# Two layernormed tiles transposed by DMA instead of TensorE, with a reordered start of the loads

## Chip, cores, metric

The kernel runs on one core of one Trainium2 chip. The time is device microseconds of one execution; several executions are taken of each kernel and the median is quoted. Before the change it was 1510.9 us (three runs, 1510.87 to 1511.14). A profile adds a trace of one execution. Its span is about 2 us shorter than the time of the same execution, so spans are compared with spans and times with times.

## The reference

The program adds three things: the input, a recurrent attention over segments, and an MLP block. The change touches only the beginning of the MLP block.

```python
x = A_x                                   # (1, 2048, 1024) bf16
xn = _layernorm(x)
out = x + _A_ref(xn, ...) + _B_ref(xn, B_w1, B_w2, B_w3, B_w4)

def _B_ref(x, w1, w2, w3, w4):            # receives xn
    h = _gelu(_layernorm(x) @ w1)         # phase one of the kernel: h
    ...                                   # shifts of h along the sequence, @ w2, phase two
    x1 = x + hs
    return x1 + _gelu(_layernorm(x1) @ w3) @ w4
```

## The kernel before

Phase one handles 16 tiles of 128 rows (0 to 15). For each tile VectorE makes the statistics, then somebody writes the twice normalized tile `xn2`. TensorE needs it transposed, as the moving operand of the product with w1. Tiles 0 to 7 are normalized by VectorE and transposed by TensorE (eight 128-column matmuls with the identity, copied by ScalarE out of PSUM, the memory that the matmuls write to). Tiles 8 to 15 are normalized by ScalarE and transposed by a DMA.

```python
ring = p0.enter_context(tc.tile_pool(name="p0ring", bufs=3))
NPE = 8
load_x(0)
for c in range(4):                                     # w1 in four quarters, 524 KB each
    nc.sync.dma_start(w1_sb[:, 2 * c:2 * c + 2, :], w1_v[:, 2 * c:2 * c + 2, :])
    if c < 2:
        load_x(1 + c)
# ... x tiles 3 to 6, w2, x tiles 7 to 9 ...

def norm_stats(n, part=None):
    # ... bn_stats, bn_aggr and ab on VectorE, rr on GpSimd ...
    if n >= NPE:
        nc.gpsimd.tensor_scalar(nm2[:], mv[:, 0:1], rr[:, 1:2], -1.0, ...)

def norm2(n, xn2T, jj):
    xn2 = ring.tile([P, D], BF16, tag="xn2")           # three slots
    if n < NPE:
        nc.vector.tensor_scalar(xn2[:, c], xts[n][:, c], ...)           # L274
    else:
        nc.scalar.activation(xn2[:], xts[n][:], ACTF.Identity, ...)     # L276
        nc.sync.dma_start_transpose(xn2T[:, jj], xn2[:])
    return xn2

def norm1(n):                                          # the once normalized tile, kept
    nc.vector.tensor_scalar(xn_keep[n // 4][:, n % 4], xts[n][:], ...)
    # ... stored to memory by GpSimd's queue ...
    load_x(n + 10)

def stage1(n0, nt, xn2T, between, j0=0):
    for co in range(KT):                               # 8 column blocks
        ps = psum.tile([P, 512], F32, tag="mm", bufs=4)
        for k in range(KT):
            nc.tensor.matmul(ps[...], w1_sb[:, k, co * P:(co + 1) * P], xn2T[...], ...)
        nc.scalar.activation(hTB[...], ps[:, :w], ACTF.Gelu_apprx_tanh)  # frees the PSUM slot
        for f in between.get(co, ()):                  # transposes, normalizations of later tiles
            f()

def prep(n):
    norm2_of(n); norm_stats(n + 1); norm1(n - 2)
```

## Time and profile before

| what | before |
|---|---|
| median time | 1510.9 us (in the later comparison of six executions 1511.02) |
| span of the profile | 1508.97 us (rounded to 1509.0 on the page) |
| TensorE at work | 99% of the span |
| first product with w1 ends | 11.98 us |
| phase two (product with w2) begins | 67.47 us |
| last matmul ends | 1505.08 us |
| from there to the end of the span | 3.89 us |

The last rows come from the trace's records of TensorE. The stretch from the end of the first product to the beginning of phase two, 55.49 us, holds everything that the change touches except the load order. It is called *the stretch* below.

One view of the kernel before that the prediction does not show is needed later: ScalarE's instructions in order of time (start, length, engine, line, what, and in brackets an idle time and its releaser).

```profile
28.80 0.38 ACT L318 ACTIVATE hTB<-ps 128x256 bf16<-128x256 f32 x1 [0.23 <-PE ps L316]
29.07 1.23 ACT L276 ACTIVATE xn<-xt,nm,rr 128x1024 bf16<-128x1024 bf16 x1
30.21 0.37 ACT L318 ACTIVATE hTB<-ps 128x256 bf16<-128x256 f32 x1
```

L318 is the copy with GELU that frees a PSUM slot. L276 is the normalization of tile 8. It begins at 29.07 in between two such copies and delays the next by 1.2 us, which four PSUM slots absorb: TensorE shows no wait there.

### The profile page before, as it was taken

Reading aid. Unit: us, or ns where it says so; the run is one execution under the profiler, and the core shown is the slowest. Engines: PE = TensorE matmul, PEld = TensorE weight load, DVE = VectorE, ACT = ScalarE, POOL = GpSimd, SP = SyncE. Lnnn points to the kernel's source line nnn. Section 1 sums busy time; section 2 is a strip of 40 time slices with the busy share of each in tenths; the row PEclk is TensorE's granted clock in tenths of the full one; section 3 lists DMA queues with packets and bytes.
Section 4 is the critical chain, followed back from the end, with each engine's and each line's share of the span. In section 5 each row is a group of like instructions: output and inputs, shape, how many; then the busy total and the mean of one; then the engine's idle time right before and its main releaser. Section 6 shows DMA issues by size and latency. Waiting matters only on the chain.

```text
span 1509.0 us, 24273 instructions
## 1 busy us (share of the span) xinstructions
PE 1499.1 (99%) x9778; PEld 804.6 (53%) x9850; DVE 544.6 (36%) x1136; ACT 504.0 (33%) x1144; POOL 175.0 (12%) x245
## 2 busy tenths in 40 slices
PE   9999999999999999999999999999999999999998
PEld 8844444445444444444466645664665455545555
DVE  8382230100020212211246624651564166516641
ACT  6533103013012011111156614650663266416630
POOL 5241020211111221100000000001000100010001
PEclk9999999999999999999999999999999999999999
DMA  8699752363345877622389957992998299918921
GB/s 303 143 273 320 216 177 90 136 203 112 126 159 149 196 247 253 217 98 84 126 224 253 243 125 178 252 241 67 240 252 203 74 227 227 214 60 199 217 48 51
DMA packets 303251, 272.41 MB, mean 181 GB/s; under 512 B 153894, under 2 KB 270152, under 8 KB 303136
## 3 DMA queue, kind: packets, MB, share of 16 engines
q1 hardware_dynamic: 281248, 189.92, 51.1%
q0 software_dynamic: 21744, 80.83, 15.7%
q8 instruction: 79, 1.29, 0.4%
q14 instruction: 36, 0.29, 0.1%
q10 hardware_dynamic: 144, 0.07, 0.0%
HBM read 190.08 MB, written 45.29 MB: 156 GB/s over the span
## 4 chain that ended last, share of the span: by engine, by line
PE 98%; DMA 1%; issue 0%; SPq 0%; DVE 0%
PE ps L654 30%; PE pso L712 15%; PE ps L593 15%; PE ps L534 13%; PE ps L560 13%; PE ps L392 4%; PE ps L316 3%; PE psO L693 2%; PE psS L669 2%; PE ps L852 1%; PE ps L484 1%; DMA PT<-Pn 1%; PE gps L463 0%; PE ps L449 0%; DMA w_sb<-in_B_w_dram 0%
## 5 line engine op out<-in xcount | busy, mean ns | idle before, releaser
L654 PE MATMUL ps<-hTb,wt 128*128 128x396 bf16 (+2 forms) x2528 | 484.8, 342 | 0.0
L654 PEld LDWEIGHTS <-wt 128*128 128x128 bf16 x2528 | 236.8, 98 | 175.4
L593 PE MATMUL ps<-wt,xT 128*128 128x512 bf16 x1003 | 220.1, 379 | 1.1
L712 PE MATMUL pso<-wo_sb,oX 128*128 128x512 bf16 (+1 forms) x972 | 208.5, 372 | 1.1
L534 PE MATMUL ps<-xn3T,w_sb 128*128 128x512 bf16 x896 | 196.2, 379 | 0.0
L560 PE MATMUL ps<-w_sb,h3T 128*128 128x512 bf16 x873 | 194.3, 379 | 1.2
L593 PEld LDWEIGHTS <-xT 128*128 128x128 bf16 x1024 | 100.2, 98 | 120.8
L535 ACT ACTIVATE h3T<-ps 128x512 bf16<-128x512 f32 x112 | 66.8, 597 | 290.4 <-PE ps L534 289.5
L712 PEld LDWEIGHTS <-oX 128*128 128x128 bf16 x992 | 96.3, 98 | 107.4
L656 ACT CAST KT<-ps 128x462 bf16<-128x462 f32 (+2 forms) x160 | 81.7, 510 | 203.1 <-PE ps L654 199.0
L560 PEld LDWEIGHTS <-h3T 128*128 128x128 bf16 x896 | 87.0, 98 | 103.4
L534 PEld LDWEIGHTS <-w_sb 128*128 128x128 bf16 x896 | 86.6, 98 | 102.1
L675 DVE TENSOR_REDUCE sums<-sm 99x4 f32<-99x396 f32 (+2 forms) x176 | 97.6, 555 | 114.3 <-ACT sm L673 114.3
L658 ACT ACTIVATE QT<-ps 128x462 bf16<-128x462 f32 (+2 forms) x160 | 83.8, 524 | 120.4 <-PE ps L654 106.1
L595 ACT CAST Vs<-ps 128x512 bf16<-128x512 f32 x64 | 37.4, 585 | 233.2 <-PE ps L593 175.0
L671 DVE TENSOR_TENSOR sm<-psS,c_mask_reg_sb 99x396 f32<-99x396 f32 x152 | 86.7, 570 | 72.6 <-PE psS L669 72.4
L599 DVE CAST Vs<-ps 128x512 bf16<-128x512 f32 x64 | 44.3, 692 | 171.6 <-PE ps L593 163.2
L673 ACT ACTIVATE sm<-sm 99x396 f32<-99x396 f32 (+2 forms) x176 | 92.8, 527 | 34.7 <-DVE sm L671 27.9
L681 DVE TENSOR_TENSOR Pn<-sm,rs 99x396 bf16<-99x396 f32 (+2 forms) x176 | 98.9, 562 | 6.8 <-DMA PT<-Pn 0.9
L719 POOL DMA_DIRECT2D out_dram<-ot x30 | 16.4, 545 | 698.9 <-DVE ot L718 693.0
L561 DVE TENSOR_TENSOR R<-ps,R 128x512 f32<-128x512 f32 x32 | 21.9, 689 | 173.5 <-PE ps L560 156.8
L718 DVE TENSOR_TENSOR ot<-pso,Rt 128x512 bf16<-128x512 f32 (+1 forms) x33 | 22.2, 675 | 170.6 <-PE pso L712 166.5
(122 smaller groups left out, 1054.1 us busy)
## 6 DMA issues: line engine op xcount, KB each, us to landing
wt<-in_A_Wq_dram SPq DMA_DIRECT2D x76, 512.0 KB
wt<-in_A_Wk_dram SPq DMA_DIRECT2D x76, 512.0 KB
wt<-in_A_Wv_dram POOLq DMA_DIRECT2D x24, 1024.0 KB, 6.5
V_scratch<-Vs SPq DMA_DIRECT2D x32, 512.0 KB
V<-V_scratch SPq DMA_DIRECT2D x40, 384.0 KB
R_scratch<-x POOLq DMA_DIRECT2D x16, 512.0 KB, 3.5
R<-R_scratch SPq DMA_DIRECT2D x16, 512.0 KB
R_scratch<-R POOLq DMA_DIRECT2D x16, 512.0 KB, 3.1
```

The costliest lines, as they stand in the source:

```text
L534: nc.tensor.matmul(ps[:].rearrange("p (n t) -> p n t", t=P), w3_sb[:, k, f * P:(f + 1) * P], xn3T[tb][:, :, k, :], start=(k == 0), stop=(k ...
L535: nc.scalar.activation(h3T[:, f, :], ps[:], ACTF.Gelu_apprx_tanh)
L560: nc.tensor.matmul(ps[:], h3T[:, f, j * P:(j + 1) * P], w4_sb[:, f, ch * 512:(ch + 1) * 512], start=(f == 0), stop=(f == FT - 1))
L593: nc.tensor.matmul(ps[:], xT[:, m4 * 4 + j, k, :], wv[:, k, :], start=(k == 0), stop=(k == KT - 1))
L654: nc.tensor.matmul(ps[:, :nb], w[:, k, hh * P:(hh + 1) * P], B["hT"][:, k, :nb], start=(k == 0), stop=(k == KT - 1))
L656: nc.scalar.copy(dst[:, hh, :], ps[:, :nb])
L658: nc.scalar.mul(dst[:, hh, :], ps[:, :nb], scale)
L671: nc.vector.tensor_tensor(sm[:T, :, :T], S3, t["mask"][:].unsqueeze(1).to_broadcast((T, 4, T)), op=ALU.add)
L673: nc.scalar.activation(e[:T, :, :T], sm[:T, :, :T], ACTF.Exp, scale=LN2)
L675: nc.vector.tensor_reduce(ss, e[:T, :, :T], axis=AX.X, op=ALU.add)
L681: nc.vector.tensor_tensor(Pn[:T, :, :T], e[:T, :, :T], rs[:T, :].unsqueeze(2).to_broadcast((T, 4, T)), op=ALU.mult)
L712: nc.tensor.matmul(self.ps[:, :self.w], self.oX[0][:, h, self.oX[1] + self.gl * P:self.oX[1] + (self.gl + 1) * P], wo_sb[:, h, self.cc], s ...
```

## The change

The intent: take 16 transposing matmuls off TensorE, which is the bound (tiles 6 and 7 by DMA, still normalized on VectorE); load x tile 2 behind w1's third quarter so that TensorE gets that quarter sooner; and record the transposes of tiles 2 and 3 one column block earlier.

```diff
-                    NPE = 8
+                    NPE = 6
...
-                        if c < 2:
-                            load_x(1 + c)
+                        if c in (0, 2):
+                            load_x(1 + c // 2)
...
-                        if n >= NPE:
+                        if n >= 8:
                             nc.gpsimd.tensor_scalar(nm2[:], ...)
...
-                        if n < NPE:
+                        if n < 8:
                             ... nc.vector.tensor_scalar(xn2[:, c], ...)
                         else:
                             nc.scalar.activation(xn2[:], ...)
+                        if n >= NPE:
                             nc.sync.dma_start_transpose(xn2T[:, jj], xn2[:])
...
-                            stage1(n - 1, 1, ..., {7 - n: [lambda n=n: tr(n, 0)], 8 - n: [lambda n=n: tr(n, 1)]}, (n - 1) % 2)
+                            stage1(n - 1, 1, ..., {6 - n: [lambda n=n: tr(n, 0)], 7 - n: [lambda n=n: tr(n, 1)]}, (n - 1) % 2)
...
-                        if n0 == 4:
-                            for c in range(4):
-                                between[1 + 2 * c // 2 + (c > 1)] += [lambda c=c: tr(6 + c // 2, c % 2)]
```

More of the change, by code (lines that the diff above doesn't have):

```diff
@@ L351 @@
                     load_consts(4)
-                    for n in range(1, NPE):
+                    for n in range(1, 8):
                         if n > 1:
@@ L361 @@
                         elif n < 4:
-                            stage1(n - 1, 1, tiles2[(n - 1) // 2 * 2], {7 - n: [lambda n=n: tr(n, 0)], 8 - n: [lambda n=n: tr(n, 1)]}, (n - 1) % 2)
+                            stage1(n - 1, 1, tiles2[(n - 1) // 2 * 2], {6 - n: [lambda n=n: tr(n, 0)], 7 - n: [lambda n=n: tr(n, 1)]}, (n - 1) % 2)
                     stage1(3, 1, tiles2[2], {0: [lambda: tr(4, 0)], 2: [lambda: tr(4, 1)], 4: [lambda: tr(5, 0)], 5: [lambda: tr(5, 1)]}, 1)
```

## The prediction

Its sum: 1510.9 - 0.89 - 0.01 = 1510.0 us. The 0.89 rests on 55.8 ns per 128-column matmul, as in the trace before (starts 55 or 56 ns apart, 48 in 2.68 us). The 0.01 assumes that swapping two loads leaves the landing of w1's fourth quarter where it was, which was my estimate from the even landings of the quarters (9.67 and 11.03 us). This quarter landed 3.34 us after the second one before the change (7.69 to 11.03).

> **What bounds the kernel now.** I read the page's engine table and its chain first, then TensorE's waits, then the chain in order of time for the first 70 us, where the whole change lies.
>
> ```profile
> PE 1499.1 (99%) x9778; PEld 804.6 (53%) x9850; DVE 544.6 (36%) x1136; ACT 504.0 (33%) x1144; POOL 175.0 (12%) x245
> ...
> PE 98%; DMA 1%; issue 0%; SPq 0%; DVE 0%
> ```
>
> TensorE is on the chain for 98% of the span. The list of its waits is nearly empty in the first 130 us:
>
> ```profile
> PE warm L333 <- DVE wz L327: 1.4, 1, 1.4
> PE ps L306 <- DMA w_sb<-in_B_w_dram: 0.3, 1, 0.3
> PE ps L306 <- ACT xn2T L296: 0.2, 1, 0.2
> ```
>
> In the whole span there is only one more, of 0.2 us. So TensorE's own work sets the end: an instruction taken off TensorE takes its own length off the time, if no wait fills the hole. What TensorE does in phase one, with the length of each piece as second number (a chain of start, length, what):
>
> ```profile
> 3.17 6.50 DMA w_sb<-in_B_w_dram
> 9.67 0.05 issue
> 9.71 1.07 PE ps L306 x16
> 10.78 0.45 PE ps L293 x8
> 11.23 0.92 PE ps L306 x16
> ...
> 26.57 0.22 PE ps L293 x4
> 26.79 0.87 PE ps L316 x8
> 27.66 0.22 PE ps L293 x4
> 27.88 1.75 PE ps L316 x16
> 29.63 0.22 PE ps L293 x4
> 29.85 0.87 PE ps L316 x8
> 30.73 0.22 PE ps L293 x4
> 30.95 36.68 PE ps L316 x336
> ```
>
> L306 is the first product with w1, row block by row block, L293 the transposes, L316 the later products. The reader is to see two things. The four L293 pieces from 26.57 on are the transposes of tiles 6 and 7, each a hole of 0.22 us in a stream that otherwise never stops. And before 9.71 the chain runs back into a load: TensorE had been waiting for the third quarter of w1 for 0.3 us.
>
> When do the quarters land? The load queue (SP) tells it, since in the built kernel every issue waits for the landing of the eighth issue before it. Counting from x tile 0, the w2 loads wait for w1's second quarter, x tile 2, w1's third quarter and w1's fourth. The last three of them:
>
> ```profile
> 8.34 0.38 SPq L244 DMA_DIRECT2D w_sb<-in_B_w_dram  x1
> 9.69 0.37 SPq L244 DMA_DIRECT2D w_sb<-in_B_w_dram  x1
> 11.05 0.37 SPq L244 DMA_DIRECT2D w_sb<-in_B_w_dram  x1
> ```
>
> So x tile 2 landed just before 8.34, the third quarter at about 9.67 and the fourth at about 11.03. A quarter (524 KB) takes 1.36 us, some 386 GB/s, and the view of stretches shows the transfers saturated (shares of about 1.0) from 3.5 to 25.5 us.
>
> [...] The trace has 0.22 us for four, or 0.45 for eight: 55.8 ns[...]. [...] In the trace the transpose issued alone at 49.99 has its traffic from 51.0 to 52.5, with a peak of 291 GB/s in a half-microsecond slice[...].
>
> **The change part by part.**
>
> *Transposes of tiles 6 and 7 off TensorE.* The built kernel has 16 matmuls and 16 weight loads fewer. On the chain they are 4 pieces of 0.2232 us (4 x 55.8 ns), together 0.89 us. The pieces after them run on at the pace of 0.109 us per 256-column matmul on either side, so nothing hides the holes: minus 0.89 us. Four copies from PSUM on ACT (0.58 us each) go too; ACT is not on the chain, so 0.
>
> *Their two DMA transposes.* The inputs are still made on VectorE:
>
> ```profile
> 23.16 0.55 DVE L274 TENSOR_SCALAR xn<-xt,mv,rr 128x1024 bf16<-128x1024 bf16 x1
> ...
> 25.88 0.55 DVE L274 TENSOR_SCALAR xn<-xt,mv,rr 128x1024 bf16<-128x1024 bf16 x1
> ```
>
> These are tiles 6 and 7, ready at 23.7 and 26.4. The transpose issued alone later in this phase shows what comes then:
>
> ```profile
> 49.99 1.23 SPq L277 DMA_TRANSPOSE xn2T<-xn  x1
> ```
>
> 1.23 us to issue, and its bytes have moved by about 52.4: 2.4 us in all. Tile 6 meets the end of the saturated stretch, so I allow it until 27.5. Tile 7 has lighter traffic (half of the engines' time from 25.5, 0.9 from 26.5) and should land at 29.0 to 29.5. TensorE needs both when it begins the product of tiles 6 and 7. That product begins after the 64 matmuls of tiles 4 and 5: it begins at 24.81 (the chain has 32 matmuls from 23.92, the first 16 of them tile 3's at 55.8 ns), and 64 x 0.109 us and the four holes end at 32.7 now, hence at about 31.8 after the change. About 2.5 us to spare: 0. The queue stays in order, but the loads of x tiles 14 and 15 were issued at 25.3 and 28.0, just after the two issues end, and tile 15 is first read at 40.8.
>
> *Third x tile behind the third quarter.* The third quarter lands where x tile 2 used to leave off plus what the swap saves, at 9.67 minus 0.68 (262 KB at 386 GB/s), so at 9.0. The wait of 0.3 us ahead of it vanishes, the 16 matmuls begin at about 9.40, and with the 8 transposes of tile 1 TensorE is done at 10.75. There it wants the fourth quarter, and the same bytes stand before that one as before the change: 11.03. Before the change TensorE came to it at 11.05, just as it landed, so no wait shows. Now a wait of 0.3 us shows. The wait moves by one quarter, gain 0.0 to 0.03 us. X tile 2 lands at about 9.70 in place of 8.3; VectorE first turns to it at 9.67, and it waits 0.28 us for x tile 3 two microseconds later anyway, so the delay of some 0.05 us is swallowed.
>
> *Transposes of tiles 2 and 3 sooner.* They move ahead by one group of 8 matmuls (0.45 us). The same instructions run, and the inputs are long there: tile 2's is ready at 12.9 and is wanted at 14.4 (14.83 less 0.45). What it buys is room for the copy of tile 2's second half, which ends at 16.34 where TensorE reads it at 16.39. No wait is shown there now: gain 0.
>
> Sum: 1510.9 - 0.89 - 0.01 = 1510.0 us, a gain of 0.06%. Behind phase one everything is released by the progress of TensorE and shifts with it.
>
> **The rivals.** *The load wait really goes.* If the fourth quarter had landed well before 11.05, the swap would save 0.3 us more: 1509.7. For it: the profile shows no wait for that quarter. Against it: the issue at 11.05 that waits for its landing. *A DMA transpose takes the place.* If tile 7 landed after 31.8, TensorE would wait for it; at 32.7 the gain is gone (1510.9), and at 34 the kernel is 1.3 us slower (1512.2). For it: tile 6 is issued into saturated traffic, and tile 7's issue stands behind it and a load in one queue. Against it: more than 2 us to spare. *A later engine or transfer swallows the shift.* TensorE shows no wait after 12 us but one of 0.2 us, so a transfer that runs on its own clock would have to be nearly late now; then anything down to no gain (1510.9). *VectorE becomes the bound early.* It is busy for 9.4 to 9.7 of 10 us up to 40 us, and a late x tile 2 could push all normalizations back; tile 2's margin of 1.5 us would have to be used up first, and the time would then be about 1510.5.
>
> **Range and chances.** The three runs of before spread over 0.27 us. The first rival makes 1509.7 and partial losses 1510.5, so 1509.6 to 1510.5 should hold 8 in 10. Two per cent are 30 us. The change touches 1 us of TensorE's work, and no rival comes near 30 us: within 2% at 0.994, 0.003 for either side.
>
> **What would show the steps right or wrong.** Right: 48 in place of 64 transposes; TensorE's load wait of about 0.3 us still there, now ahead of the last 16 matmuls of L306; no wait ahead of the product of tiles 6 and 7; the next phase beginning about 0.9 us before its present 67.6. Wrong: a wait of TensorE for a DMA transpose near 32 us; the last 16 L306 matmuls beginning clearly before 11.0; VectorE's second tile statistics starting late by more than 0.3 us and TensorE waiting at a transpose; or a start of the next phase shifted by other than 0.8 to 1.0 us with the end shifted by another amount.

## More of the kernel before

Note the pools: `xn2` lives in a ring of three slots (buffers that are used again and again; a new tile must wait until the last reader of its slot is done), and the product's PSUM ring ("mm") has four.

## The result, and the profile after

The changed kernel took 1512.51 us in the median. Its six executions fall in two groups: 1511.77, 1511.99, 1512.40 and 1512.61, then 1514.79 (the profiled one) and 1514.82. The kernel before, measured on the same chip in the same rounds, had a median of 1511.02 (1510.82 to 1512.17). A ratio is the mean time of one kernel's runs over that of the other's of the same rounds, so it is not quite the ratio of the medians. Here it is 1.0011, with a 95% interval of 0.9998 to 1.0024: within 2%, as predicted, but 2.5 us above the predicted time, and even the fastest execution lies above the predicted range. The interval touches 1, so the times alone hardly show the loss. The profile shows it piece by piece.

The engine table of the page after, and the shares of the chain that ended last:

```profile
PE 1503.9 (99%) x9834; PEld 804.6 (53%) x9834; DVE 544.3 (36%) x1136; ACT 502.3 (33%) x1140; POOL 174.9 (12%) x245
...
PE 98%; DMA 1%; DVE 0%; issue 0%; POOL 0%; ACT 0%; POOLq 0%; DVEq 0%
```

Weight loads went from 9850 to 9834, as counted: 16 fewer, and ScalarE's instructions from 1144 to 1140. (The matmul counts, 9778 and 9834, can't be compared: the trace before lacks some records.) TensorE is still the bound, but GpSimd and ScalarE now stand in the list of the chain, which was not so before. TensorE's waits after (line waited in, releaser, total us, times, longest):

```profile
PE ps L317 <- ACT hTB L319: 2.0, 1, 2.0
PE warm L334 <- DVE wz L328: 1.4, 1, 1.4
PE psO L691 <- DMA PT<-Pn: 0.8, 1, 0.8
```

The first line is new. It is a wait of 2.0 us in the product with w1 (L317), and the releaser is a ScalarE copy, not a DMA. The load wait of before is gone from the list in this profile: TensorE started that product later, at 7.76 instead of 7.45, and the fourth quarter came earlier, at 10.75 instead of 11.03. The chain in order of time tells the story of the 2.0 us:

```profile
23.42 0.55 DVE xn L274
...
23.99 4.68 DMA xn2T<-xn
...
28.77 0.55 DVE xn L274
29.32 0.61 DVE st L262
...
29.96 0.22 DVE mv L263
...
30.20 0.23 DVE ab L264
...
30.58 0.88 POOL rr L265
...
31.55 0.28 POOL nm L267
...
31.85 0.05 ACT xn L276
...
33.00 0.37 ACT hTB L319
...
33.41 11.65 PE ps L317 x90
```

Read from the top: VectorE normalizes tile 6 (23.42). Its DMA transpose takes 4.68 us. Only when that has landed does VectorE normalize tile 7 (28.77). Then come the statistics of tile 8 on VectorE and GpSimd, ScalarE's normalization of tile 8, a ScalarE copy, and only then TensorE. VectorE's own view of the same time:

```profile
25.44 0.69 DVE L259 BATCH_NORM_STATS2 st<-xt 128x6 f32<-128x512 bf16 x1
28.77 0.55 DVE L274 TENSOR_SCALAR xn<-xt,mv,rr 128x1024 bf16<-128x1024 bf16 x1 [2.65 <-DMA xn2T<-xn]
```

VectorE stood still for 2.65 us, waiting for tile 6's DMA transpose before it wrote tile 7. The load queue's view after:

```profile
23.99 1.43 SPq L278 DMA_TRANSPOSE xn2T<-xn  x1
25.55 0.54 SPq L234 DMA_DIRECT2D xt<-in_A_x_dram  x1
29.35 1.40 SPq L278 DMA_TRANSPOSE xn2T<-xn  x1
```

The queue issued in the recorded order (23.99, 25.55, 29.35). Tile 7's transpose was issued at 29.35, where the prediction had its input ready at 26.4. Pairing issues with their completions in the trace, tile 6 landed at 28.68 and tile 7 at 32.23. ScalarE's view, against the one of before:

```profile
27.98 0.38 ACT L319 ACTIVATE hTB<-ps 128x256 bf16<-128x256 f32 x1 [0.49 <-PE ps L317]
31.85 1.24 ACT L276 ACTIVATE xn<-xt,nm,rr 128x1024 bf16<-128x1024 bf16 x1 [3.49 <-POOL nm L267]
33.00 0.91 ACT L319 ACTIVATE hTB<-ps 128x256 bf16<-128x256 f32 x3
```

ScalarE has tile 8's normalization next in its order, waits 3.49 us for it, and only at 33.00 makes three copies in a row. Until then the four PSUM slots are full and TensorE can't write.

TensorE stood from 31.44 to 33.41, and that had a sequel. Stretches of half a microsecond with TensorE's busy time, granted clock, DMA share and GB/s:

```profile
34.00:34.50 0.50, 0.50 (x7) 1.00 0.29 67
34.50:35.00 0.50, 0.50 (x6) 0.68 1.27 289
35.00:35.50 0.50, 0.50 (x4) 0.50 1.18 291
37.50:38.00 0.50, 0.50 (x5) 0.50 1.04 341
38.00:38.50 0.50, 0.50 (x6) 0.91 0.56 189
```

The third number from the right is the granted clock that the trace records, as a share of TensorE's full speed. From 34.67 to 38.09, for 3.413 us, it is at half: 256-column matmuls start 0.213 us apart there, and 0.109 us apart before and after. About half of 3.413 us, 1.7 us, is lost by my estimate. What decides whether a stop is followed by half clock is not shown here. In the changed kernel half clock follows a stop of 1.98 us; after stops of 1.89 us (e2_filled), 0.96 us (e6_tile8_later) and 0.75 us (e1b_both_own_place) in the experiments below none follows.

Where the 3.65 us between the two profiled executions are:

| piece | before | after | difference |
|---|---|---|---|
| start to end of first product | 11.98 | 11.78 | -0.20 |
| the stretch, to phase two | 55.49 | 58.23 | +2.74 |
| phase two to last matmul | 1437.61 | 1438.27 | +0.66 |
| last matmul to end of span | 3.89 | 4.35 | +0.46 |
| span | 1508.97 | 1512.63 | +3.65 |

(The differences are rounded one by one.)

The stretch splits into -0.89 (16 transposes), -0.17 (a gain at tile 2 that was predicted as 0, below), +1.98 (the wait), +0.17 (what a stop costs TensorE beyond the idle time, taken from the experiments below), and +1.65 left over, which matches the 1.7 of the half clock. Without the half clock it would be +1.09.

Where does the stop of VectorE come from? The list of the built program's instructions names what tile 7's normalization waits for. First the kernel before, then after:

```
54 L274 TensorScalarPtr xn_577<-xt_145,mv_555,rr_557 128x1024 [waits PE_49,Pool_49]
54 L274 TensorScalarPtr xn_578<-xt_145,mv_555,rr_557 128x1024 [waits DMAHW6_49,Pool_49]
```

Before, tile 7 took the ring slot that TensorE had last read (tile 4's, by its address). After, it has the same address as tile 6, so it must wait until tile 6's DMA transpose has been read out; DMAHW6 is that transpose's completion. My reading is that a slot comes free in recording order: the last reader of tile 6 is its DMA, recorded together with its normalization, whereas TensorE's transposes of tiles 4 and 5 are recorded further down. So the slot that is free first in the recording is the one that is free last in time. The addresses and the wait are facts of the build; the reason for the choice is inferred from them.

### The profile page after: what moved, and what is told of

Its sections match the earlier page's. It is cut to its first block, busy times and chain, and to the rows that moved or that the text cites. A ratio compares the mean times of both kernels' runs of the same rounds, so it can differ in the third digit from the quotient of the medians.

```text
span 1512.6 us, 24316 instructions
## 1 busy us (share of the span) xinstructions
PE 1503.9 (99%) x9834; PEld 804.6 (53%) x9834; DVE 544.3 (36%) x1136; ACT 502.3 (33%) x1140; POOL 174.9 (12%) x245
## 4 chain that ended last, share of the span: by engine, by line
PE 98%; DMA 1%; DVE 0%; issue 0%; POOL 0%; ACT 0%; POOLq 0%; DVEq 0%
PE ps L652 30%; PE pso L710 15%; PE ps L591 15%; PE ps L532 13%; PE ps L558 13%; PE ps L390 4%; PE ps L317 3%; PE psO L691 2%; PE psS L667 2%; PE ps L850 1%; PE ps L482 1%; DMA PT<-Pn 1%; PE gps L461 0%; PE ps L447 0%; PE warm L334 0%; DMA xn2T<-xn 0%
```

## The experiments

All twelve gave correct outputs and were timed. The quoted expectations name the theories by letters that belong to the state of the argument then; the text here names them by content. The theories were: the shared slot makes the loss; the DMA transposes are too slow in any case; ScalarE's order passes VectorE's delay on to TensorE; the half clock makes the spread of times; two more transfers lengthen the program's end. The rival to all was that the 1.5 us are scatter of the measurement.

### Tile 7 in a place of its own (e1_own_place)

```diff
-xn2 = ring.tile([P, D], BF16, tag="xn2")
+xn2 = xn_keep[3][:, 3] if n == 7 else ring.tile([P, D], BF16, tag="xn2")
```

The borrowed place is that of tile 15's kept normalization, which is written much later.

> The changed kernel, but the normalized tile 7 is written into storage of its own (the place of tile 15's kept copy, free until about 43 us) instead of the ring slot that it shares with tile 6. Theory A (shared slot): VectorE no longer waits for the landing of tile 6's DMA transpose, tile 7's transpose is issued at about 26.5 in place of 29.35 us, TensorE has no wait at the product of tiles 6 and 7, no half-clock stretch follows, and the time is 1511.0 - 0.9 = 1510.1 us (1509.8 to 1510.5). Theory B (slow transfers): the transposes land late because of the saturated queues, whatever the slot; tile 7's then lands after 31.5 us, TensorE still waits 1 us or more, and the time stays at 1511.5 or more.

Measured: 1511.31 us (1511.06 to 1512.17) against 1511.30 for before in the same rounds, ratio 0.9997 (0.9984 to 1.0009). In VectorE's view tile 7 no longer waits, and its transpose is issued 2.7 us after tile 6's:

```profile
27.52 0.55 DVE L274 TENSOR_SCALAR xnk<-xt,mv,rr 128x1024 bf16<-128x1024 bf16 x1
```

TensorE has no wait at this product and no half clock, and the stretch is 54.43 us. That is 55.49 - 0.89 - 0.17, the whole gain. So without the shared slot neither VectorE's stop nor TensorE's wait is there. Two reservations belong to it. The time missed the expected 1510.1 and only came back to that of before; in this execution the first loads were late (first product ended at 13.63) and the end took 4.35 us. And tile 7 landed as late as 33.07: TensorE did not wait for it because it was itself 1.85 us later than in the changed kernel.

### Tiles 6 and 7 both in places of their own (e1b_both_own_place)

```diff
-xn2 = ring.tile([P, D], BF16, tag="xn2")
+xn2 = xn_keep[3][:, n - 4] if n in (6, 7) else ring.tile([P, D], BF16, tag="xn2")
```

> As the run before, but tiles 6 and 7 both get storage of their own, so that ScalarE's normalization of tile 8 need not wait for tile 6's transpose either. Theory A: same time as the run before, within 0.2 us (1510.1 us), since ScalarE has 3 PSUM buffers in hand. If ScalarE's wait of some 0.6 us for tile 6's transpose matters there, this one is faster by that. Theory B: 1511.5 us or more.

Measured: 1511.45 us (1511.22 to 1512.15), ratio 0.9998, so the expected 1510.1 was missed here too. Here the first product ended at 12.43, and TensorE met tile 7's transpose:

```profile
PE ps L317 <- ACT xn L276: 0.8, 1, 0.8
...
24.18 1.38 SPq L278 DMA_TRANSPOSE xn2T<-xnk  x1
25.74 1.10 SPq L234 DMA_DIRECT2D xt<-in_A_x_dram  x1
26.94 1.53 SPq L278 DMA_TRANSPOSE xn2T<-xnk  x1
```

The wait list puts the 0.8 us down to a normalization on ScalarE, that of tile 9, which ended at 32.79. TensorE needs nothing of it: ScalarE had made seven of the eight copies of the product before by 31.64, so there were free PSUM slots. What TensorE did need was tile 7: issued at 26.94, landed at 32.80, and TensorE went on at 32.84. The two ends fall together, and the list names the wrong one. The stretch is 55.35, which is 54.43 plus the wait of 0.75 and 0.17 for the stop. So the slow transposes are a cause of their own: 5.01 us for tile 6, 5.86 for tile 7, with a load of an x tile between them.

### The changed kernel with TensorE kept busy (e2_filled, e2b_filled_other_bank)

Nine matmuls of zeros (nine times 0.216 us, the spacing of 512-column matmuls in phase two of the trace before) stand ahead of the product of tiles 6 and 7, to see whether the half clock goes when TensorE does not idle. First they write to a slot of the product's PSUM ring:

```diff
+if n0 == 6:
+    ps = psum.tile([P, 512], F32, tag="mm", bufs=4, name="fill")
+    for i in range(9):
+        nc.tensor.matmul(ps[:], wz[:, :P], wz[:], start=(i == 0), stop=(i == 8))
```

> The changed kernel, with nine matmuls of 512 columns on zeros (9 x 0.216 = 1.94 us) put ahead of the product of tiles 6 and 7, where TensorE stood idle for 1.98 us. The outputs are unchanged. Theory C (the idle stretch costs twice, once as a wait and once as a stretch at half the clock in some executions): no stretch at half clock in the profile, the executions near 1514.8 us vanish, all lie at 1511.8 to 1512.4 us, that is 1511.0 - 0.9 + 2.0. Rival: the spread from 1511.8 to 1514.8 us comes from elsewhere (the transposes of the attention stage); then some executions are still at 1514 us or above.

This missed: 1514.48 us (1514.36 to 1518.61), ratio 1.0026. The filling itself had to wait:

```profile
PE fill L379 <- ACT hTB L319: 1.9, 1, 1.9
```

It did not wait for tile 7 at all, but for a PSUM slot. That pointed to ScalarE's copies, which I had not thought of, as the door that was shut. No half clock shows in this profile in spite of 1.89 us of idle time (the 87 matmuls from 35.51 on take 9.66 us, 0.109 us apart). Two executions that were not profiled took 1516.74 and 1518.61; their cause is open.

The second attempt writes the same nine matmuls into the other PSUM ring, that of the transposes (`psum0`, tag "tr").

> The changed kernel, with nine matmuls on zeros (1.94 us) ahead of the product of tiles 6 and 7, this time into the transposes' PSUM buffer, so that they need not wait for ScalarE as those of the first filling did. Theory C: TensorE is busy through the stretch, the profile shows no stretch at half clock, all executions lie within 1 us of 1512.1 us (1511.0 - 0.9 + 2.0) and none reaches 1514. Rival: the executions near 1514.8 us do not come from the clock; then one or two of six are there again.

Measured: 1513.07 us (1512.48 to 1513.51) against 1511.72 for before in these rounds, ratio 1.0007. TensorE ran without a stop through the time in question, at full clock (the 101 matmuls from 34.03 on take 11.19 us, again 0.109 us apart). None of its executions reached 1514, as expected, though two of the five (1513.34 and 1513.51) lie over 1 us from the expected 1512.1, which left out the longer end of the program (below). The spread of the five is 1.0 us, where the changed kernel's six spread over 3.1 us. That fits the half clock as the reason for the two groups of times, but it is weak support: single slow executions come without such a stop as well (1517.05 among eleven of the kernel before; 1513.74 in e4_loads_behind, whose profiled execution has no stop). Half clock in the midst of TensorE's work is shown in one profile only; for the other execution at 1514.8 it is inferred.

### Tile 8's normalization later on ScalarE (e6_tile8_later)

```diff
-between[1 + 2 * (n0 == 4)] += [lambda n0=n0: prep(n0 + 4)]
-between[4 + 2 * (n0 == 4)] += [lambda n0=n0: prep(n0 + 5)]
+between[1 + 6 * (n0 == 4)] += [lambda n0=n0: prep(n0 + 4)]
+between[4 + 3 * (n0 == 4)] += [lambda n0=n0: prep(n0 + 5)]
```

The changed kernel with its shared slot, but with the whole preparation of tiles 8 and 9 (their normalizations on ScalarE, and VectorE's work recorded with them) behind the last block of tiles 4 and 5.

> The changed kernel with its shared slot, but ScalarE's normalization of tiles 8 and 9 is put behind the last PSUM copy of the product of tiles 4 and 5 instead of between its copies. Theory D (TensorE stood still because ScalarE, held up at tile 8's normalization, did not empty the PSUM buffers): VectorE still waits some 2.6 us for tile 6's transpose, but TensorE's wait falls from 2.0 us to about 0.8 us, when tile 7's transpose lands (about 32.2), and no half-clock stretch follows; time about 1511.0 - 0.9 + 0.8 = 1510.9 us, no execution above 1513. Rival (TensorE waited for tile 7's transpose alone): its wait stays at 2.0 us.

Measured: 1512.18 us (1511.34 to 1514.58), ratio 1.0008. The wait in the profile:

```profile
PE ps L317 <- DMA xn2T<-xn: 1.0, 1, 1.0
```

It is halved, from 1.98 to 0.96 us, and its releaser is now the DMA transpose of tile 7 (landed 32.26, TensorE on at 32.31). So about 1.0 of the 2.0 us came through ScalarE's order, and the rest is tile 7's late landing. The stretch is 55.58, that is 54.43 plus 0.96 and 0.19. The expectation that no execution lies above 1513 missed: two did, 1513.48 and 1514.58. The profiled one did not, so their cause stays open.

### The loads behind the transposes (e4_loads_behind)

```diff
-load_x(n + 10)
+if n == 5:
+    load_x(14)
+if n != 4:
+    load_x(n + 10)
```

On top of both tiles in places of their own, x tile 14 is no longer issued between the two transposes but after both.

> Tiles 6 and 7 in storage of their own, and the loads of x tiles 14 and 15 issued behind tile 7's transpose instead of between and after the two transposes. In the run with both in storage of their own, tile 7's transpose took 5.9 us (26.9 to 32.8) and TensorE waited 0.75 us for it. Theory B (other transfers queued around it make a transpose slow): tile 7's now lands 1 us or more sooner after its issue (under 5 us), TensorE has no wait at the product of tiles 6 and 7, and from the first product's end to the next phase's beginning the profile shows 54.6 us (55.5 of before less 0.9). Time: 0.9 us under the kernel before in the same rounds, give or take the scatter of the start. Rival (the transpose is slow by itself when it follows another one): tile 7's takes 5.5 us or more again.

Measured: 1511.50 us (1510.14 to 1513.74) against 1511.72, ratio 1.0000. Tile 7's transpose took 4.39 us in place of 5.86 and landed at 31.57, and TensorE did not wait. The stretch is 54.43, the full gain. The end of the span took 4.69 us, 0.79 more than before, and this ate most of it: the time is 0.2 us under the kernel before, not the expected 0.9.

### Only tile 6 by DMA (e5_one_tile)

```diff
-xn2 = ring.tile([P, D], BF16, tag="xn2")
+xn2 = xn_keep[3][:, 2] if n == 6 else ring.tile([P, D], BF16, tag="xn2")
...
-if n >= NPE:
+if n == 6 or n >= 8:
     nc.sync.dma_start_transpose(xn2T[:, jj], xn2[:])
...
+if n0 == 4:
+    for c in range(2):
+        between[1 + 2 * c] += [lambda c=c: tr(7, c)]
```

> Only tile 6 is transposed by DMA (from storage of its own), tile 7 stays on TensorE. Tile 6's transpose lands near 29 us and is wanted near 32: no wait. Eight transposes of 55.8 ns are removed: 0.45 us less than the kernel before in the same rounds; in the profile 55.05 us from the first product's end to the next phase, no wait of TensorE between.

Measured: 1511.20 us (1510.66 to 1511.87), ratio 0.9995. The stretch is 55.66, where 55.05 was expected. My placement of tile 7's transposes was too early: TensorE waited 0.61 us at 26.11 for VectorE's normalization. The run says little about one tile against two. Its end, with one transfer more instead of two, took 3.81 us.

### The load order alone (e3_order_only)

```diff
-if c < 2:
-    load_x(1 + c)
+if c in (0, 2):
+    load_x(1 + c // 2)
```

This is the kernel before with only these lines changed.

> The kernel before, with nothing changed but the order of loads: third x tile behind w1's third quarter. Theory (the wait only moves to the fourth quarter): 1511.0 us, same as before within 0.1; the third quarter lands about 0.7 us sooner relative to the second, the fourth at the same distance from the second as before. Rival (the wait goes): 0.3 us faster, 1510.7 us.

Measured: 1510.68 us (1510.36 to 1512.09) against 1511.30, ratio 0.9994 (0.9982 to 1.0007). The wait for w1 is 0.5 us, and it stands at 10.70, ahead of the last 16 matmuls of the first product, where before it stood at 9.40, ahead of the 16 before these. The product ended 0.95 us after the fourth quarter landed (11.16 and 12.11), exactly as in the kernel before (11.03 and 11.98). The wait moves and nothing is gained. The 0.6 us in the medians is of the size of the next run's difference.

### The kernel before, unchanged (e7_before_again)

> The kernel before, unchanged, as a run of its own: how far two equal kernels lie apart in this measure, and a second profile of the start. Expected: ratio 1.0000, within 0.3 us; in its profile TensorE waits for a quarter of w1 (third or fourth) and its first product ends some 0.95 us after the fourth quarter has landed, as in the kernels with the changed order of loads.

Measured: 1511.00 us (1510.33 to 1511.78, five executions) against 1511.40 (nine executions) for the same kernel in the same rounds, ratio 0.9997. So 0.4 us between two medians means nothing. In its profile the third quarter came later and the product ended at 12.51 instead of 11.98: the first loads alone scatter by half a microsecond here. Over all the profiles the end of the first product lies between 11.69 and 13.63. The stretch is 55.49, the same to the last digit, which is why it is the yardstick.

### Transposes of tiles 2 and 3 sooner, alone (e10_sooner_only)

```diff
-stage1(n - 1, 1, ..., {7 - n: [lambda n=n: tr(n, 0)], 8 - n: [lambda n=n: tr(n, 1)]}, (n - 1) % 2)
+stage1(n - 1, 1, ..., {6 - n: [lambda n=n: tr(n, 0)], 7 - n: [lambda n=n: tr(n, 1)]}, (n - 1) % 2)
```

> The kernel before, with nothing changed but the place of the transposes of tiles 2 and 3 among the matmuls. My prediction said 0 for this part; the profiles since then say that TensorE lost some 0.17 us at tile 2, since 48 matmuls of 55.8 ns took 2.84 in place of 2.68 us. Expected: in the profile that stretch takes 2.68 us and from the first product's end to the next phase 55.3 us in place of 55.5; the time 0.2 us under the kernel before. Rival: no change, 55.5 us.

Measured: 1511.16 us (1510.45 to 1511.56) against 1511.40, ratio 0.9998. The stretch is 55.32, 0.17 less than before. The chain shows where, first in the kernel before:

```profile
15.50 0.22 PE ps L293 x4
15.72 0.67 PE ps L316 x12
16.39 0.00 issue
16.39 2.17 PE ps L316 x36
```

And with the transposes sooner:

```profile
15.77 0.22 PE ps L293 x4
16.00 2.68 PE ps L316 x48
```

Before, 48 matmuls take 0.67 + 2.17 = 2.84 us and the chain is cut at 16.39, where TensorE reads the copy of tile 2's second half that had just been made. Now they take 2.68, which is 48 times 55.8 ns. There had been a wait that no list of waits names: the matmul at 16.39 starts 0.22 us after the one before it in place of 0.056, 0.17 us late.

### Two transfers more, in the kernel before (e8_two_more)

```diff
-nc.sync.dma_start(m0[:], A_mem0[0])
+for i in range(3):
+    nc.sync.dma_start(m0[:, (0, 256, 512)[i]:(256, 512, 1024)[i]], A_mem0[0][:, (0, 256, 512)[i]:(256, 512, 1024)[i]])
```

A small load far from both ends of the program is cut in three, so that this queue issues two transfers more, as in the changed kernel.

> The kernel before with one small load (16 KB, near 128 us, where nothing waits for it) cut into three, so that the load queue carries two transfers more, as the changed kernel does. Theory E (two more transfers turn the round of eight semaphores by two, and the queue's waits at the end of the program then come behind the last output instead of before it): the time from TensorE's last matmul to the end of the span grows from 3.9 to 4.3 us or more (changed kernel 4.3, the one with the loads behind 4.65), the time by 0.4 to 0.7 us over the kernel before. Rival (the longer tail comes from the shift in phase one): 3.9 us.

Measured: 1512.30 us (1511.85 to 1512.89) against 1511.40, ratio 1.0006. The end, from the last matmul to the end of the span, took 4.72 us in place of 3.89, and the stretch is 55.49 as before, so the longer end needs no shift in phase one. In the traces of the kernel before and the changed one the load queue's transfers report on eight completion semaphores in turn, and at the end the SP engine waits for all eight in the same order. In the kernel before the last output transfer is on the seventh of them, so one wait follows it, of 0.08 us (1507.18 to 1507.26). Shifted by two it is on the first, and seven waits follow, 0.55 us in the changed kernel (1510.37 to 1510.92). Over all fourteen profiles the end takes 3.89 us where the queue issues as many transfers as before (four profiles), 3.80 and 3.81 where it issues one more, and 4.35 to 4.72 where it issues two more (eight): six of these lie at 4.35 or 4.36, and in the other two, this run and e4_loads_behind, one of the last waits took 0.3 us longer.

### All the repairs together (e9_best)

On top of the loads behind the transposes, the small load goes to GpSimd's queue, so that the load queue has only one transfer more than before:

```diff
-nc.sync.dma_start(m0[:], A_mem0[0])
+nc.gpsimd.dma_start(m0[:], A_mem0[0])
```

> Tiles 6 and 7 in storage of their own, the loads of x tiles 14 and 15 behind tile 7's transpose, and one small load (the 16 KB of the memory rows) moved to GpSimd's queue, so that the load queue carries one transfer more than before instead of two. Theory E: from the last matmul to the end 3.85 us. With theories A and B: no wait of TensorE near 32 us, 54.4 us from the first product's end to the next phase. Sum against the kernel before in the same rounds: 0.89 (transposes) + 0.17 (sooner transposes of tiles 2 and 3) = 1.0 us less; this should beat both kernels. If it is not at least 0.5 us faster, a cost is still missing in the account.

Measured: 1510.19 us (1509.92 to 1511.05) against 1511.40 for before (1510.95 to 1511.84), ratio 0.9994 (0.998 to 1.0007). In the medians this is 1.2 us below the kernel before and 0.8 below its second measurement (1511.00). The interval still reaches 1, so five executions don't prove it. The profile fits it: span 1508.2 against 1509.0 and 1509.2, an end of 3.80 us, and a stretch of 54.73. What is left is a wait of 0.14 us for tile 7, whose transpose still took 4.97 us (26.50 to 31.47).

| kernel | median, before in the same rounds | the stretch | wait at tiles 6/7 | the end |
|---|---|---|---|---|
| before (first profile) | 1511.02 | 55.49 | 0 | 3.89 |
| changed | 1512.51, 1511.02 | 58.23 | 1.98 | 4.35 |
| e1_own_place | 1511.31, 1511.30 | 54.43 | 0 | 4.35 |
| e1b_both_own_place | 1511.45, 1511.30 | 55.35 | 0.75 | 4.35 |
| e6_tile8_later | 1512.18, 1511.72 | 55.58 | 0.96 | 4.36 |
| e4_loads_behind | 1511.50, 1511.72 | 54.43 | 0 | 4.69 |
| e9_best | 1510.19, 1511.40 | 54.73 | 0.14 | 3.80 |
| e10_sooner_only | 1511.16, 1511.40 | 55.32 | 0 | 3.89 |

The stretch and the end together account for most of the distances between the medians. For e2b_filled_other_bank (stretch 56.37, end 4.35) they make 0.88 + 0.46 = 1.34 us, and 1.35 was measured; for the changed kernel without its half clock 1.09 + 0.46 = 1.55, measured 1.49; for e4_loads_behind -1.06 + 0.79 = -0.27, measured -0.22. The worst in this table is e1_own_place: -1.06 + 0.46 = -0.60, measured +0.01. So where the load queue issues two transfers more, what is won in phase one is for a good part lost again in the last waits of the program.

## Why the prediction was right or wrong

- **Transposes of tiles 6 and 7 off TensorE, -0.89: right.** The instructions left as counted, and wherever no wait fills the hole (e1_own_place, e4_loads_behind) the stretch is shorter by 0.89 and the 0.17 of e10_sooner_only, exactly.
- **"Their two DMA transposes", 0: this is the step that failed.** It forecast no wait ahead of the product of tiles 6 and 7; TensorE stopped for 1.98 us there. Three of its terms fell. First, "ready at 23.7 and 26.4": tile 7 was ready at 29.3, because it had been given tile 6's slot and waited for the DMA that read it. I had compared the order of instructions on the engines but not what they wait for in the built program, where the new wait stands in plain sight. Second, the "2.4 us in all" was worked out from the transpose at 49.99, the one I picked because it stood alone. From issue to completion that one took 2.74 us, and it is the shortest of the eight in phase one of the trace before; the others took 2.84 to 6.84 us. The allowance for tile 6 (27.5) was thus too small by 1.2 us even though I had seen that it met traffic. Tile 7's own transpose took 2.88 us in the changed kernel, within its allowance of 2.6 to 3.1; issued at 26.5 to 28.1, in the runs without the shared slot, it took 4.39 to 5.86. Third, "about 2.5 us to spare" was compared with tile 7's landing alone. VectorE's delay also went through tile 8's statistics to ScalarE, whose order put tile 8's normalization ahead of the copies that free PSUM. That took another 1.0 of the 1.98 us.
- **The rival "A DMA transpose takes the place": its mechanism was a part of this one, and it was given too little weight.** It named the traffic and the queue, and put a landing at 34 at 1.3 us slower than before. TensorE did go on at 33.41. What it did not contain is the shared slot, the way through ScalarE, and the half clock after the stop, an estimated 1.7 us in the one profile that shows it.
- **"Third x tile behind the third quarter", 0.0 to 0.03: right.** The wait moved by one quarter and the product ended 0.95 us after the fourth quarter in either order (e3_order_only). The 0.3 us that was to show in the changed kernel did not show in its profile, where TensorE started later and the quarter landed earlier; it is there in e3_order_only with 0.5 us.
- **"Transposes of tiles 2 and 3 sooner", 0: the mechanism was right, the size was off.** The prediction saw that the copy ended at 16.34 where it is read at 16.39 and took this as just in time. It was just too late: 0.17 us (e10_sooner_only). That two events stand next to each other can be the sign of a wait.
- **"Behind phase one everything ... shifts with it": wrong at the very end.** Two transfers more on the load queue cost 0.46 us in the changed kernel's profile (0.83 in e8_two_more) through the order of the last waits. No step of the sum had the end of the program in it.
- **The chances were right** (no change by 2%), **the range too narrow.** It was built on 0.27 us of scatter among three runs; the kernel before itself spread over 1.3 us in the comparison with the changed kernel, and from 1510.68 to 1517.05 in another.

Open are what decides whether a stop is followed by half clock, the reason why a DMA transpose takes 4 to 6 us amid other transfers (moving a load behind them helped, from 5.86 to 4.39 and 4.97 us, but not down to 2.7), the two slow executions of e6_tile8_later, and a wait of 0 to 0.8 us in the attention stage (L691 in the list after) that comes and goes from profile to profile and makes most of the +0.66 in the ledger.

## What to carry to other kernels

Before work moves from one engine to another, look up in the built program what the next writer of each ring slot waits for: an operation recorded earlier can be one that finishes later. Here the ring handed out such a slot, and VectorE stood still for 2.65 us. Take the cost of a transfer from those in the trace that stand in similar traffic, all of them, and not from the cleanest one (here 2.74 us, where the others took 2.84 to 6.84). A delay of an engine off the critical path is not bounded by its own consumer: follow it through every engine that runs in order, down to the buffers that the bound engine needs (here about 1.0 of TensorE's 1.98 us came that way).
